# The second half's channels in a folded order, with `w1` copied once into that order in DRAM

## The chip, the cores and the metric

The kernel runs on one core of one Trainium2 chip. The metric is the time of one execution on the device in microseconds (us), the median of several runs. An execution that the hardware profiler recorded gives the profile; it has a time of its own.

## The reference

One transformer block on x of 2048 rows and 512 channels, all in float32. A vector `c` gives six modulation vectors of 512 channels: shift, scale and gate for each of the two halves.

```python
mod = (_silu(c) @ w_mod).reshape(c.shape[0], 6, 1, -1)
sa, ca, ga, sb, cb, gb = (mod[:, 0], mod[:, 1], mod[:, 2], mod[:, 3], mod[:, 4], mod[:, 5])
h = _layernorm(x, axis=-1) * (1 + ca) + sa
x = x + ga * _A_ref(h, A_wqkv, A_wo)          # linear attention, 32 heads of 16
h = _layernorm(x, axis=-1) * (1 + cb) + sb
x = x + gb * _B_ref(h, B_w1, B_b1, B_w2)      # mish(h @ w1 + b1) @ w2
```

`w1` is 512 x 1792, `w2` 1792 x 512. The first half ends with `x1 = x + ga * attention`. The second half is a layer norm of x1, two matrix products with Mish between them, and an addition to x1.

## The kernel before

**Tiling.** Rows are cut into four blocks of 512 (`b` 0 to 3), each of four tiles of 128 rows (`t`). A tile has 128 partitions and 512 columns. Channels are cut into four chunks of 128 (`j`). Every float32 operand of a product is split into a high and a low part of reduced precision, and a product is three matmuls (high by high, high by low, low by high). Most products are Strassen-like: of a 2 x 2 partition of the operands seven products are made from sums and differences (`m1` to `m7`, or `a11 b11`, `s1 t1` and so on), so VectorE makes many sums and low parts, and ScalarE the high parts.

**Stages.** From the start to about 120 us: layer norms of the blocks of x, `k` for blocks 0 to 3 (`k_unit`), and the Gram products (`g_unit`). SyncE's queue is an in-order list of loads: those of x for blocks 2 and 3 come from `load_x` in the loop `for b in range(1, NB)`, and block 3 goes through DRAM (`xd`) and back as 32 x 32 squares (`load_squares`, `y_x`). Then `q` (`q_sevens`), during which `mod_side` loads rows of `w_mod` (L155, two loads a step) and reduces each on VectorE against the activated `c` three steps later (`mod_col`, L232): column i of `mc` is the modulation of 128 channels. Rows 8 to 15 of the 24 tiles are loaded singly, 16 to 23 in pairs in the order 20 to 23, 16 to 19. Then attention (`attend`, whose reciprocals `rden` go through DRAM), `o_unit`, and x1 is stored to DRAM as `x1d` (L920).

In these parts instructions are emitted in an order fixed by `tick`, one step of every running helper per unit of TensorE's work; each engine executes its own list in order.

**The second half**, from about 187 us on, is emitted by `drive`. It keeps a main stream (pairs of products with `w1`, Mish after them) and a fill stream (`unit`, products with `w2`). All other work is jobs with due times. `drive` models every engine's clock, picks the job that can start first, and among those the one due first; the table `T` holds lead times, due times and costs. A DMA job without a fixed queue goes to SyncE or POOL, whichever the model finds free first. The order of the instructions is thus fixed when the kernel is built, and a change of `T` changes it.

**Ways of the data in the second half.** Blocks 0 and 1 are normalized on ScalarE (`norm_first`, `norm_each`) and turned by TensorE (`transpose_f`, `tp_op`). Blocks 2 and 3 are normalized in place (`norm_job`), stored to DRAM (`to_dram`, tiles `nd`), read back as squares into `yd` (`squares_job`, L1727) and turned by VectorE, which transposes 32 x 32 blocks (`turn_job`). Here `x1d` and `nd` have the shape [4, 512, 128]: chunk by chunk, so a row of a chunk is 512 bytes, and one row of a square is a run of 32 numbers, 128 bytes:

```python
yield (y[32 * c:32 * (c + 1), :].rearrange("q (m r) -> q m r", r=32),
       bass.AP(tensor=d.tensor, offset=d.offset + 512 * P * j0 + 32 * c, ap=[[P, 32], [32 * P, n], [1, 32]]))
```

The results have channels on partitions. They go three ways. For blocks 0, 1 and the first column of the second pair (block L = 2) `result_job` gates them (L1618), transposes them on VectorE into `turned` (L1629), and POOL adds them into `x1d` by four accumulating DMAs a job (L1635). `copy_out` (L1695) then copies a finished block from `x1d` to `out`. For block 3 `load_r` reads squares of x1 into `rq` (L1594), VectorE adds the transposed result (`rows_half`, L1660), and squares go straight to `out` (L1664). The last product, `m3` of block 2, is made in row order: VectorE multiplies it by the gate and adds it to `rows01`, rows of `x1d` loaded at L1892, and POOL stores them (L1928). Each engine's list is in order, so an instruction that waits for a DMA holds up what stands behind it, for example the low parts at L1270.

`w1` is loaded in `rows` (L797, the first two groups) and `rows_job` (L1288), `w2` in `w2_blocks`, `blocks_job` and `sums_job`; splits and differences of `w2` are stored to DRAM (`w2d`, `w2t`) and read again in `right_job` (L1446). Tiles named `wt_m` are these.

Of the kernel before, what the change touches and what calls it, by code (L numbers as in the profile page):

```python
# [8 lines left out]
F32 = mybir.dt.float32  # L9
F32R = mybir.dt.float32r  # L10
AF = mybir.ActivationFunctionType
ALU = mybir.AluOpType
# [17 lines left out]
 'urgent': 3.1,  # L30
 'store_later': 10.8,
 'row_lead': 12.6,
 'columns': 94.0,
 'column_lead': 27.7,
 'rows_early': 12.0,
 'lead_a': 4,
 'lead_l': 14,
 'lead_r': 14,
# [4 lines left out]
 'blocks_early': 13.3,  # L43
# [3 lines left out]
 'early_at': -0.3,  # L47
 'norm_due': 62.5,
# [10 lines left out]
 'left_early': 19.1,  # L59
 'right_due': 2.0,  # L60
 'right_early': 13.2,
 'sum_due': 1.0,
 'sum_early': 11.2,
 'pace_a': 5.6,
 'pace_l': 3.2,
 'pair_l': 16.4,
 'seq_0': 'ABCD.E.FG',
 'seq_l': 'AB.CD.E.F.G.',
 'copy_due': 10.0,
 'result_due': 5.0,  # L70
 'soon': 10.2,
 'r_due': 5.3,
 'out01': 54.8,
 'sum_store': 8.1,
 'half_due': 8.9}

@with_exitstack
def block_kernel(ctx: ExitStack, tc: tile.TileContext, x, wqkv, wo, w1, b1t, w2, c, wmodt, out):
# [18 lines left out]
    def f32(t):  # L97
        return t.bitcast(F32)

# [53 lines left out]
    def load_wmod(i):  # L153
        wm[i] = sb(f"wm_{i}")
        sp.dma_start(wm[i], wmodt[P * i:P * (i + 1), :])  # L155
# [138 lines left out]
    def strips(d, t):  # L294

        return d[:, P * t:P * (t + 1), :].rearrange("j p r -> p j r")
# [13 lines left out]
    def strip_squares(y, d, j0):  # L310

        n = y.shape[1] // 32
        for c in range(4):
            yield (y[32 * c:32 * (c + 1), :].rearrange("q (m r) -> q m r", r=32),
                   bass.AP(tensor=d.tensor, offset=d.offset + 512 * P * j0 + 32 * c, ap=[[P, 32], [32 * P, n], [1, 32]]))
# [363 lines left out]
    def w2_blocks(g):  # L679
# [8 lines left out]
        act.activation(first[:, 0, :], r[0][:, 0:H], AF.Copy)  # L688
        act.activation(h, r[1], AF.Copy)
        yield  # L690
        dve.tensor_tensor(first[:, 1, :], r[0][:, 0:H], f32(first[:, 0, :]), op=ALU.subtract)
        dve.tensor_tensor(l, r[1], f32(h), op=ALU.subtract)
# [98 lines left out]

    def rows(g, wait):

        r = [sb(f"w1p_{g}_{i}", F32, (P, 4, P)) for i in range(2)]
        for i in range(2):
            f = 2 * g + i
            sp.dma_start(r[i], w1[:, P * f:P * (f + 1)].rearrange("(k p) f -> p k f", p=P))  # L797
# [25 lines left out]
    op_rows, rows_d = {}, {}  # L823

    early_rows = [rows(g, 3 * g + 1) for g in range(2)]

    for b in range(1, NB):
# [89 lines left out]
    def x1_store(b, t, queue=pool):  # L917
        if b not in x1d:
            x1d[b] = drp.tile([4, 512, P], F32, name=f"x1d_{b}")
        queue.dma_start(strips(x1d[b], t), xt["r", b, t].rearrange("p (j r) -> p j r", r=P))  # L920
# [15 lines left out]
    def norm_first(t):  # L936
# [9 lines left out]
        ln_apply("n", 0, t, xt["r", 0, t], v, act)  # L946

    def norm_each(b, t):
# [15 lines left out]
        ln_apply("n", b, t, xt["r", b, t], v, act)  # L964
# [139 lines left out]
    LATE = T['late']  # L1104
    QUEUE = {SP: sp, POOL: pool, ACT: act}
# [173 lines left out]
    def rows_job(g, due, l=0):  # L1279
# [5 lines left out]
        def load(q, i):  # L1285
            r[i] = sb(f"w1p_{l}_{g}_{i}", F32, (P, 4, P))
            f = 2 * g + i
            q.dma_start(r[i], w1[:, P * f:P * (f + 1)].rearrange("(k p) f -> p k f", p=P))  # L1288
# [66 lines left out]
    def blocks_job(g):  # L1355
# [12 lines left out]
        def upper(i):  # L1368
            if i == 0:
                st[0] = sb(f"b11_{g}", F32R, (P, 2, H))  # L1370
                act.activation(st[0][:, 0, :], r[0][:, 0:H], AF.Copy)
            else:
                st[1] = sb(f"b2_{g}_0", F32R)
                act.activation(st[1], r[1], AF.Copy)

        def lower(i):
            if i == 0:
                dve.tensor_tensor(st[0][:, 1, :], r[0][:, 0:H], f32(st[0][:, 0, :]), op=ALU.subtract)
                right[0, "m1", g] = [st[0][:, k, :] for k in range(2)]
            else:  # L1380
                st[2] = sb(f"b2_{g}_1", F32R)
                dve.tensor_tensor(st[2], r[1], f32(st[1]), op=ALU.subtract)
# [15 lines left out]
    def sums_job(g):  # L1398
# [13 lines left out]
        def diff(n):  # L1412
            if n == 0:
                t[0], t[1] = [sb(f"t{m}_{g}") for m in (12, 34)]
            b11, b12, b21, b22 = [v[:, c:c + H] for v in (r[0], r[1]) for c in (0, H)]
            t1, t2, t3, t4 = t[0][:, 0:H], t[0][:, H:D], t[1][:, 0:H], t[1][:, H:D]
# [167 lines left out]
    def load_r(L, n):  # L1584
# [4 lines left out]
        for c in range(4):  # L1589
            def go(q, c=c):  # L1590
                if c == 0:
                    alloc()
                sq, rows_ = list(strip_squares(rq[L, n], x1d[L + n], 0))[c]
                q.dma_start(sq, rows_)  # L1594
            yield dma_(go, [("rq", L, n)] if c == 3 else (), size=2 * LATE)

# [15 lines left out]
    def result_job(L, place, n, c, us, needs, frees=()):  # L1612
# [13 lines left out]
        def turn_(i):  # L1626
            if turned[L, n] is None:
                turned[L, n] = big.tile([P, 4 * 512], F32, tag="Y", name=f"turned_{L}_{n}", bufs=YS)
            dve.transpose(turned[L, n][:, 1024 * c + 512 * i:1024 * c + 512 * (i + 1)], q[i])  # L1629

        for i in range(2):
            yield d_(lambda i=i: turn_(i))
        both = turned[L, n][:, 1024 * c:1024 * (c + 1)]
        for k, (sq, rows_) in enumerate(strip_squares(both, x1d[L + n], 2 * c)):
            yield dma_(lambda q, sq=sq, rows_=rows_: q.dma_start(rows_, sq, accum_op=ALU.add),  # L1635
                       [("sum", L, n, c)] if k == 3 else (), queue=POOL)


    def rows_half(L, place, c, i, us, keep):
# [15 lines left out]
        v = lambda: rq[L, 1][:, 512 * (2 * c + i):512 * (2 * c + i + 1)]  # L1655
# [4 lines left out]
        yield d_(lambda: dve.tensor_tensor(v(), v(), q[1], op=ALU.add), needs=[("rq", L, 1)])  # L1660
# [32 lines left out]
    def copy_out(q, b, c0, c1):  # L1693

        q.dma_start(out_rows(b)[:, P * c0:P * c1].rearrange("p (j r) -> p j r", r=P),  # L1695
                     x1d[b][c0:c1].rearrange("j p r -> p j r"))
# [272 lines left out]
```

## Time and profile before

| what | us |
|---|---|
| median of 3 runs | 492.26 |
| lowest and highest of them | 487.68, 492.45 |
| the profiled execution's own time | 495.81 |
| its span, first to last instruction | 494.1 |
| TensorE busy | 474.2 |
| VectorE busy | 418.3 |
| ScalarE busy | 321.1 |
| POOL busy | 177.5 |

The span is cut into 40 slices on the page, each 12.35 us. TensorE's clock was granted in full but for short stretches (mean 0.986). The DMA engines moved 97.24 MB in 115200 packets, 66641 of them under 512 bytes. PE is TensorE, PEld its weight loads, DVE VectorE, ACT ScalarE, SP SyncE; a name with a q behind it is that engine's queue of DMA issues. A line such as `PE m L128 <- DVE l_m_5l L1270: 7.9, 1, 7.9` says that TensorE's instruction of line 128 that writes `m` waited for VectorE's of line 1270 that writes `l_m_5l`: 7.9 us in total, once, the longest 7.9. In a stretch of time stand its length, then each engine's busy time in it with the number of its instructions, the granted clock, the DMA engines' busy share and the rate in GB/s; where transfers overlap on an engine the share can pass 1. A row of the DMA issues ends with the size of one and the median time from issue to landing.

### The profile page before, as it was taken

Reading aid. Unit: us, or ns where it says so; the run is one execution under the profiler, and the core shown is the slowest. Engines: PE = TensorE matmul, PEld = TensorE weight load, DVE = VectorE, ACT = ScalarE, POOL = GpSimd, SP = SyncE. Lnnn points to the kernel's source line nnn. Section 1 sums busy time; section 2 is a strip of 40 time slices with the busy share of each in tenths; the row PEclk is TensorE's granted clock in tenths of the full one; section 3 lists DMA queues with packets and bytes.
Section 4 is the critical chain, followed back from the end, with each engine's and each line's share of the span. In section 5 each row is a group of like instructions: output and inputs, shape, how many; then the busy total and the mean of one; then the engine's idle time right before and its main releaser. Section 6 shows DMA issues by size and latency. Waiting matters only on the chain.

```text
span 494.1 us, 7316 instructions
## 1 busy us (share of the span) xinstructions
PE 474.2 (96%) x2300; PEld 387.7 (78%) x2300; DVE 418.3 (85%) x818; ACT 321.1 (65%) x583; POOL 177.5 (36%) x245
## 2 busy tenths in 40 slices
PE   8999999999999999999999999989999999999936
PEld 6778887877877888888888778868888888888835
DVE  7989988999789798998888799968975689899734
ACT  6768586756445979779889696655565648443400
POOL 4583320000113431345421235522312266862722
PEclk9999999999999999999999999989999999999969
DMA  8705597145784536579989769983234399999996
GB/s 310 286 2 122 176 151 234 43 129 171 263 197 126 167 108 229 182 265 358 276 241 274 252 203 217 302 295 121 71 122 146 92 246 218 272 284 218 242 129 135
DMA packets 115200, 97.24 MB, mean 197 GB/s; under 512 B 66641, under 2 KB 89049, under 8 KB 115162
## 3 DMA queue, kind: packets, MB, share of 16 engines
q0 software_dynamic: 38672, 44.06, 39.3%
q1 hardware_dynamic: 72120, 51.93, 36.7%
q10 hardware_dynamic: 4370, 0.79, 0.9%
q8 instruction: 18, 0.29, 0.3%
q14 instruction: 20, 0.16, 0.1%
HBM read 65.81 MB, written 31.46 MB: 197 GB/s over the span
## 4 chain that ended last, share of the span: by engine, by line
PE 59%; DMA 16%; DVE 9%; issue 6%; ACT 5%; POOL 3%; SPq 2%; ACTq 0%; POOLq 0%; DVEq 0%
PE p_a L1487 15%; DMA x1d<-turned 6%; PE p_s L1487 6%; PE pa L1572 5%; PE pc L1572 3%; PE o L128 3%; PE o L126 3%; PE pq_a L464 3%; PE o L127 3%; DMA wt_m<-w2t 2%; SPq L322 2%; PE pd L1572 2%; DMA w2t<-t_5l 2%; DMA w1p<-in_w_dram 1%; PE pk L128 1%
## 5 line engine op out<-in xcount | busy, mean ns | idle before, releaser
L1446 POOL DMA_DIRECT2D wt_m<-w2t x35 | 27.6, 965 | 54.8 <-PE p_a L1487 10.6
L1511 ACT ACTIVATE u_a<-c_a,b1c 128x512 f32<-128x512 f32 x42 | 30.2, 718 | 16.3 <-DVE c_a L1508 16.3
L1635 POOL DMA_DIRECT2D x1d<-turned x24 | 34.9, 2468 | 15.7 <-DVE turned L1629 9.9
L1502 ACT ACTIVATE u<-p_a 128x512 f32<-128x512 f32 x42 | 24.9, 593 | 24.0 <-PE p_a L1487 23.7
L1508 DVE TENSOR_TENSOR c_a<-p_s,u 128x512 f32<-128x512 f32 x28 | 19.2, 685 | 11.1 <-PE p_s L1487 6.2
L1446 POOL DMA_DIRECT2D wt_m<-w2d x17 | 15.7, 1063 | 15.6 <-PE pa L1572 9.2
L920 POOL DMA_DIRECT2D x1d<-r x16 | 12.3, 769 | 24.1 <-DVE r L924 15.3
L895 POOL DMA_DIRECT2D rden_d<-rden x2 | 1.4, 714 | 48.2 <-DVE rden L893 48.2
L1461 DVE TENSOR_TENSOR u_a<-u_a,u_a 128x512 f32<-128x512 f32 x28 | 18.1, 681 | 0.0
L256 POOL TENSOR_TENSOR rs_n<-rs_n,half 128x1 f32<-128x1 f32 x16 | 9.9, 634 | 17.8 <-DVE rs_n L282 9.5
L355 ACT ACTIVATE e_k<-pk 128x512 f32<-128x512 f32 x15 | 8.9, 591 | 10.7 <-PE pk L128 10.6
L1288 POOL DMA_DIRECT2D w1p<-in_w_dram x12 | 10.4, 864 | 9.9 <-PE p_a L1487 5.9
L1607 ACT ACTIVATE U<-pa,mc 128x512 f32<-128x512 f32 x10 | 6.8, 681 | 10.9 <-PE pa L1572 10.6
L907 DVE SCALAR_TENSOR_TENSOR q<-q,rd 128x512 f32<-128x512 f32 x16 | 10.5, 684 | 3.8 <-DMA rd<-rden_d 3.8
L256 POOL TENSOR_TENSOR rs_x<-rs_x,half 128x1 f32<-128x1 f32 (+1 forms) x10 | 7.8, 783 | 15.8 <-DVE rs_x L251 14.6
L367 POOL DMA_DIRECT2D ku<-ku x8 | 7.1, 886 | 17.1 <-DVE ku L358 17.1
L358 DVE SCALAR_TENSOR_TENSOR ku<-e_k,relu_k 128x512 f32<-128x512 f32 x15 | 10.7, 712 | 3.0 <-ACT relu_k L356 2.9
L358 DVE SCALAR_TENSOR_TENSOR q<-e_q,relu_q 128x512 f32<-128x512 f32 x16 | 10.7, 685 | 2.1 <-ACT relu_q L356 2.1
L1508 DVE TENSOR_TENSOR c_a<-p_a,u 128x512 f32<-128x512 f32 x14 | 9.6, 683 | 3.2 <-PE p_a L1487 2.1
L1539 ACT ACTIVATE u_a<-p_a,b1c 128x512 f32<-128x512 f32 x14 | 9.6, 683 | 4.1 <-PE p_a L1487 3.6
L1660 DVE TENSOR_TENSOR rq<-rq,t 128x512 f32<-128x512 f32 x4 | 2.6, 675 | 9.5 <-DMA rq<-x1d 9.5
L232 DVE SCALAR_TENSOR_TENSOR wm<-wm,sc_row 128x512 f32<-128x512 f32 x16 | 10.5, 676 | 0.0
(1504 smaller groups left out, 1898.3 us busy)
## 6 DMA issues: line engine op xcount, KB each, us to landing
wt_m<-w2t POOLq DMA_DIRECT2D x35, 256.0 KB, 6.4
wm<-in_wmodt_dram SPq DMA_DIRECT2D x24, 256.0 KB, 5.1
wt_m<-w2t SPq DMA_DIRECT2D x17, 256.0 KB, 8.0
wt_m<-w2d POOLq DMA_DIRECT2D x17, 256.0 KB, 6.6
r<-in_x_dram SPq DMA_DIRECT2D x16, 256.0 KB, 3.2
x1d<-r POOLq DMA_DIRECT2D x16, 256.0 KB, 3.1
w2d<-b SPq DMA_DIRECT2D x16, 256.0 KB, 7.2
x<-in_x_dram SPq DMA_DIRECT2D x15, 256.0 KB, 4.7
```

The costliest lines, as they stand in the source:

```text
L126: pe.matmul(o, st[0], mv[0], start=start, stop=False)
L128: pe.matmul(o, st[1], mv[0], start=False, stop=stop)
L256: pool.tensor_tensor(y, y, half[:, lo:hi], op=ALU.pow)
L358: dve.scalar_tensor_tensor(dst, e, 1.0, r, op0=ALU.min, op1=ALU.add)
L1446: q.dma_start(f32(v), (w2d if src == "w2d" else w2t)[g][:, :, part, :])
L1461: dve.tensor_tensor(get(d), u, v, op=o)
L1487: pe.matmul(p, st, mv, start=onto is None and c == 0 and i == 0, stop=c == 1 and i == 2, skip_group_check=onto is not None)
L1502: act.activation(t["u", n], t["pa"], AF.Copy)
L1508: dve.tensor_tensor(t[key], t[p], t["u", n], op=ALU.add)
L1511: act.activation(u, t[key], AF.Mish, bias=b1c[:, f:f + 1])
L1572: pe.matmul(o, st[:, cs], mv, start=not onto and n == 0 and k == 0, stop=n == G - 1 and k == 2, skip_group_check=onto)
L1635: yield dma_(lambda q, sq=sq, rows_=rows_: q.dma_start(rows_, sq, accum_op=ALU.add), [("sum", L, n, c)] if k == 3 else (), queue=POOL)
```

## The change

Natural channel 128 c + 32 x + r (c and x from 0 to 3, r from 0 to 31) gets the place 128 x + 32 c + r: the folded order. Chunk x of the second half then holds, on partition 32 c + r, channel 128 c + 32 x + r.

- `x1d` and `nd` become plain [512, 512] tensors in natural order, stored in rows of 2 KB. A load of squares takes, for one c, 128 consecutive channels of each row: 512 bytes a run, 512 runs a load (2048 before), and the four chunks lie beside each other in each partition.
- Sums: for blocks 0 and 2 each `result_job` adds its two chunks, runs of 256 bytes, 512 a DMA; for block 1 the second of the two jobs adds all four chunks, runs of 512 bytes. 20 accumulating DMAs take the place of 24.
- Block 3: `rows_half` stores to `out` in four DMAs of 512-byte runs after the last of its four additions, in place of sixteen of 128-byte runs, each four after their own addition.
- The last product's rows: whole rows of `x1d` (four loads and four stores of 256 KB, with the second half of each row's columns, in folded view, added to). The rows now need both sums of block 2, and the copy of that block's first 256 columns to `out` falls away.
- `copy_out` copies 1 MB from one plain tensor to another.
- ScalarE and VectorE read and write through views that fold: the normalized blocks 0 and 1, the splits and differences of `w2`, the last rows.
- The modulation of the second half (loads `wm` 12 to 23) is read from `w_mod` in folded order, four groups of 32 rows a load.
- `w1` is copied in DRAM into `w1d` with its rows folded: four copies on SyncE's queue, one in each step of the loop's first turn (b = 1), right behind the load of a tile of x of block 3; `rows` and `rows_job` load from `w1d`.
- `T` has new values (one, `add`, is new: the modelled cost of a sum).

```diff
+    def nat(t, h=None):
+        v = t.rearrange("p (c x r) -> p x c r", c=4, r=32)
+        return v if h is None else v[:, 2 * h:2 * h + 2]
+    def lin(t):
+        return t.rearrange("p (x c r) -> p x c r", c=4, r=32)
+    def chunk(y, x):
+        return y.rearrange("q (m s) -> q m s", s=P)[:, :, 32 * x:32 * (x + 1)]
...
     def load_wmod(i):
         wm[i] = sb(f"wm_{i}")
-        sp.dma_start(wm[i], wmodt[P * i:P * (i + 1), :])
+        if i < 12:
+            sp.dma_start(wm[i], wmodt[P * i:P * (i + 1), :])
+        else:
+            r0 = 512 * (i // 4) + 32 * (i % 4)
+            sp.dma_start(wm[i], bass.AP(tensor=wmodt.tensor, offset=wmodt.offset + 512 * r0,
+                                        ap=[[512 * P, 4], [512, 32], [1, 512]]))
...
-            nd[key, b] = drp.tile([4, 512, P], F32, name=f"{key}d_{b}")
-        queue.dma_start(strips(nd[key, b], t), v.rearrange("p (j r) -> p j r", r=P))
+            nd[key, b] = drp.tile([512, D], F32, name=f"{key}d_{b}")
+        queue.dma_start(nd[key, b][P * t:P * (t + 1), :], v)
...
+    def strip_squares(y, d, c, lo=0, hi=P):
+        return (y[32 * c:32 * (c + 1), :].rearrange("q (m s) -> q m s", s=P)[:, :, lo:hi],
+                d[:, P * c + lo:P * c + hi].rearrange("(m q) s -> q m s", q=32))
...
+    w1d = drp.tile([D, F], F32, name="w1d")
+    def fold_rows(c, queue):
+        queue.dma_start(w1d.rearrange("(k c r) f -> c k r f", c=4, r=32)[c],
+                        w1.rearrange("(c k r) f -> c k r f", c=4, r=32)[c])
...
             if b + 2 < NB:
                 load_x(b + 2, t)
...
+            if b == 1:
+                fold_rows(t, sp)
...
-        ln_apply("n", b, t, xt["r", b, t], v, act)
+        ln_apply("n", b, t, nat(xt["r", b, t]), lin(v), act)
...
-            dve.transpose(turned[L, n][:, 1024 * c + 512 * i:1024 * c + 512 * (i + 1)], q[i])
+            dve.transpose(chunk(turned[L, n], 2 * c + i), q[i])
...
-        for k, (sq, rows_) in enumerate(strip_squares(both, x1d[L + n], 2 * c)):
-            yield dma_(lambda q, sq=sq, rows_=rows_: q.dma_start(rows_, sq, accum_op=ALU.add),
-                       [("sum", L, n, c)] if k == 3 else (), queue=POOL)
+        if n and c:
+            return
+        lo, hi = (0, P) if n else (64 * c, 64 * (c + 1))
+        for k in range(4):
+            def put(q, k=k):
+                sq, rows_ = strip_squares(turned[L, n], x1d[L + n], k, lo, hi)
+                q.dma_start(rows_, sq, accum_op=ALU.add)
+            yield dma_(put, [("sum", L, n, c)] if k == 3 else (), [("t", L, n, 1)] if n else (), queue=POOL, size=ADD)
...
-        for n in range(4):
+        for n in range(4) if c == 0 and i else ():
             def put(queue, n=n):
-                sq, rows_ = list(squares(v(), out_rows(L + 1), H * c + P * i))[n]
+                sq, rows_ = strip_squares(rq[L, 1], out_rows(L + 1), n)
                 queue.dma_start(rows_, sq)
-            yield dma_(put, queue=(SP, ACT)[c])
+            yield dma_(put, (), [("v", 0, 0), ("v", 1, 0), ("v", 1, 1)], queue=(SP, ACT)[n % 2])
...
-                    for t in range(2):
-                        r0 = P * (2 * i + t)
-                        q.dma_start(rows01[i][:, t, :].rearrange("p (j r) -> p j r", r=P),
-                                     x1d[L][2:4, r0:r0 + P, :].rearrange("j p r -> p j r"))
-                add_job(iter([dma_(lambda q: copy_out(q, L, 0, 2), (), [("sum", L, 0, 0)])]), now[0] + 20)
+                    q.dma_start(rows01[i], x1d[L][P * i:P * (i + 1), :])
...
-                            q.dma_start(out[512 * L + P * t:512 * L + P * (t + 1), H:D], rows01[t // 2][:, t % 2, :])
+                            q.dma_start(out[512 * L + P * t:512 * L + P * (t + 1), :], rows01[t])
```

Of `T`, among others: `blocks_early` 13.3 to 19.3, `row_lead` 12.6 to 15.5, `lead_l` 14 to 16, `lead_r` 14 to 13, `left_early` 19.1 to 16.4, `sum_early` 11.2 to 14.0, `norm_due` 62.5 to 60.3, `pair_l` 16.4 to 15.1, `half_due` 8.9 to 7.8, `r_due` 5.3 to 5.5, and `seq_l`, the order of products and fills in the last seven pairs, from `AB.CD.E.F.G.` to `AB.CD.E.FG..`.

More of the change, by code (lines that the diff above doesn't have):

```diff
@@ L46 @@
  'early_due': 96.7,
- 'early_at': -0.3,
- 'norm_due': 62.5,
+ 'early_at': -1.0,
+ 'norm_due': 60.3,
  'norm_at': 18.7,
@@ L918, in x1_store @@
         if b not in x1d:
-            x1d[b] = drp.tile([4, 512, P], F32, name=f"x1d_{b}")
-        queue.dma_start(strips(x1d[b], t), xt["r", b, t].rearrange("p (j r) -> p j r", r=P))
+            x1d[b] = drp.tile([512, D], F32, name=f"x1d_{b}")
+        queue.dma_start(x1d[b][P * t:P * (t + 1), :], xt["r", b, t])
     def o_post(p, b, t):
@@ L1592, in go @@
                     alloc()
-                sq, rows_ = list(strip_squares(rq[L, n], x1d[L + n], 0))[c]
-                q.dma_start(sq, rows_)
-            yield dma_(go, [("rq", L, n)] if c == 3 else (), size=2 * LATE)
+                q.dma_start(*strip_squares(rq[L, n], x1d[L + n], c))
+            yield dma_(go, [("rq", L, n)] if c == 3 else (), size=LATE)
     def out_rows(b):
@@ L1882, in fill_stream @@
                 for b in range(2):
-                    add_job(iter([dma_(lambda q, b=b: copy_out(q, b, 0, 4),
-                                       (), [("sum", 0, b, c) for c in range(2)])]), now[0] + T['out01'])
+                    add_job(iter([dma_(lambda q, b=b: copy_out(q, b),
+                                       (), [("sum", 0, 0, 0), ("sum", 0, 0, 1)] if b == 0 else [("sum", 0, 1, 0)],
+                                       size=8 * LATE)]), now[0] + T['out01'])
             if l == L and (name, g) == ("m6", ORDER[L][0]):
```

103 lines of the change are left out of this document (48 added, 55 removed).

## The prediction

> **What bounds the kernel now.** I read the head of the page, then the waits of TensorE, then stretches of time around each wait, then each engine's own order at those places.
>
> ```profile
> span 494.1 us, 7316 instructions
> PE 474.2 (96%) x2300; PEld 387.7 (78%) x2300; DVE 418.3 (85%) x818; ACT 321.1 (65%) x583; POOL 177.5 (36%) x245
> PE m L128 <- DVE l_m_5l L1270: 7.9, 1, 7.9
> PE pc L1572 <- DVE l_m_0l L1270: 2.1, 1, 2.1
> PE o L128 <- DVE qs_2l L140: 1.0, 1, 1.0
> ```
>
> TensorE is busy for 96%. All that can be won without taking matmuls away is its 494.1 - 474.2 = 19.9 us of idle time, and what the clock loses after it. One wait is 7.9 us, one 2.1, one 1.0. The stretches (columns: length, busy time of PE, PEld, DVE, ACT, POOL with counts, granted clock, DMA share, GB/s):
>
> ```profile
> 326.50:329.40 2.90, 0.78 (x5) 0.32 (x3) 0.69 (x1) 2.76 (x5) 0.72 (x1) 1.00 1.04 373
> 329.40:333.44 4.04, 4.04 (x10) 2.85 (x11) 2.61 (x5) 0.63 (x1) 1.14 (x2) 0.58 0.53 170
> 360.00:380.00 20.00, 20.00 (x90) 16.55 (x89) 12.59 (x22) 13.06 (x23) 4.74 (x7) 1.00 0.35 111
> 471.60:479.40 7.80, 0.00 (x0) 0.00 (x0) 1.92 (x4) 0.00 (x0) 0.27 (x1) 0.61 0.88 115
> 479.40:483.63 4.23, 4.21 (x19) 4.21 (x20) 4.23 (x8) 0.00 (x0) 2.63 (x4) 0.50 1.00 201
> 483.63:489.20 5.57, 5.56 (x46) 5.36 (x45) 2.41 (x7) 0.00 (x0) 1.69 (x3) 1.00 0.94 183
> 489.20:494.10 4.90, 0.00 (x0) 0.00 (x0) 0.85 (x2) 0.00 (x0) 0.54 (x1) 0.98 0.11 39
> ```
>
> After each stop the clock is granted by half for a while: 19 matmuls take 4.2 us at 0.50, where 46 like them take 5.57 at 1.00, so 19 cost 2.3; 1.9 us more are lost. Likewise 10 matmuls take 4.04 us at 333, against 90 in 20.00 us, 2.2 for ten; 1.8 lost. The last stop thus costs 7.9 + 1.9 = 9.8 us, the one at 327 2.1 + 1.8 = 3.9. Elsewhere, as from 360 to 380, TensorE has no hole. The last 4.9 us are the last tile's way out.
>
> What makes the last stop? VectorE's and SyncE's orders:
>
> ```profile
> 467.30 0.71 DVE L1649 SCALAR_TENSOR_TENSOR q<-pa,mc,T 128x512 f32<-128x512 f32 x1
> 477.48 0.69 DVE L1660 TENSOR_TENSOR rq<-rq,t 128x512 f32<-128x512 f32 x1 [9.47 <-DMA rq<-x1d]
> 478.71 0.65 DVE L1270 TENSOR_TENSOR l_m_5l<-u_a,l_m_5h 128x512 fp32r<-128x512 f32 x1
> 441.27 28.21 SPq L1594 DMA_DIRECT2D rq<-x1d  x4
> 466.70 11.88 DMA x1d<-turned
> ```
>
> TensorE wants `l_m_5l`. It needs nothing of `rq`, but stands behind L1660 on VectorE, which waits 9.47 us for `rq`. Four loads of `rq` keep SyncE's queue for 28 us: 2048 runs of 128 bytes each, while the sums `x1d<-turned`, 1024 runs each, share the DMA engines.
>
> **The change, part by part.**
>
> ```profile
> ku<-ku POOLq DMA_DIRECT2D x8, 256.0 KB, 4.6
> w1p<-in_w_dram SPq DMA_DIRECT2D x12, 256.0 KB, 5.3
> x1d<-turned POOLq DMA_DIRECT2D x24, 128.0 KB, 9.1
> x1d<-r POOLq DMA_DIRECT2D x16, 256.0 KB, 3.1
> out_dram<-rows POOLq DMA_DIRECT2D x4, 128.0 KB, 2.8
> rows<-x1d POOLq DMA_DIRECT2D x4, 128.0 KB, 3.4
> 464.28 5.48 POOL L1635 DMA_DIRECT2D x1d<-turned  x4 [1.30 <-DVE turned L1629]
> 479.13 2.90 POOL L1892 DMA_DIRECT2D rows<-x1d  x4 [9.36 <-DMA x1d<-turned]
> 490.41 0.54 POOL L1928 DMA_DIRECT2D out_dram<-rows  x1 [1.98 <-DVE rows L1925]
> ```
>
> Loads of `rq`: 512 runs of 512 bytes. By run count the 28.2 us of issue become 7.1 and the last lands about 441.3 + 7.1 + 5.3 (the `w1p` row, 512-byte runs) = 454; with no gain from longer runs it stays at 477. VectorE comes to L1660 at 468.0, so the stop goes if more than 9.5 of the 28.2 us go: a third saved, 9.4, all but does it. Taken: gone, -9.8.
>
> Sums: 24 issues of 1024 runs become 20 of 512 (16 of 256 bytes, 4 of 512). The nearest rows are the 128-byte sums (9.1 us for 128 KB) and the accumulation `ku` in 2 KB runs (4.6 for 256 KB, 2.3 for 128); 256 bytes lie nearer the first row. I take 5 to 6. Some run ahead of the stop at 327, which comes through a buffer that a store still holds. Bounds: 0 to -3.9; taken half, -2.0.
>
> Squares of `n` (L1727), stores of `n` and `x1` and copies to `out` keep their place and get fewer runs; TensorE waits for none of them: 0. Folded views on ScalarE and VectorE move as many elements; no row shows such a view, but the stage from 190 on is TensorE's (the 360 row: VectorE 12.6 of 20), so a tenth more on each would stay covered: 0.
>
> The tail: the four last stores carry 256 KB where 128 were. By the two rows (3.1 against 2.8) +0.3. Their rows now also wait for both halves of the sums; the last sums are issued from 464.3 and land at 478.6 (466.70 + 11.88). At half that flight they land near 473; four `rows` loads, 2.9 us of issue and 3.4 of flight, are there by 480, about when TensorE would end (489.2 - 9.8 = 479.4): 0. The four additions into `rq` now leave in four stores of 256 KB (sixteen of 64 before), none before the last addition is done; what queues behind that on SyncE and ScalarE is nothing else, and with VectorE free from 468 on it is over before TensorE's end: 0. The 512 KB copy of the third block's first half to `out` falls away, off every path: 0.
>
> `w1d` and `wm`: four copies (0.92 MB each, with x(3,1) to x(3,3) between them on SyncE's queue), and loads `wm` 12 to 23, whose DRAM side now has an outermost dimension of 4. What that costs is seen at `rden_d`, the one DMA here with 4 outermost, which runs alone from 180.6 to 181.8; beside it `wm` loads as they are now:
>
> ```profile
> 121.00:122.00 1.00, 1.00 (x7) 0.81 (x6) 0.98 (x2) 0.97 (x2) 0.00 (x0) 1.00 1.06 408
> 180.60:181.80 1.20, 1.20 (x8) 1.03 (x7) 1.20 (x4) 0.00 (x0) 0.93 (x1) 1.00 0.23 53
> 179.02 0.57 SPq L895 DMA_DIRECT2D rden_d<-rden  x1
> 119.00 0.80 SPq L155 DMA_DIRECT2D wm<-in_wmodt_dram  x2
> 121.40 0.80 SPq L155 DMA_DIRECT2D wm<-in_wmodt_dram  x2
> 122.77 0.86 SPq L155 DMA_DIRECT2D wm<-in_wmodt_dram  x2
> 124.99 0.88 SPq L155 DMA_DIRECT2D wm<-in_wmodt_dram  x2
> 137.15 0.69 DVE L232 SCALAR_TENSOR_TENSOR wm<-wm,sc_row 128x512 f32<-128x512 f32 x1
> 138.98 0.69 DVE L232 SCALAR_TENSOR_TENSOR wm<-wm,sc_row 128x512 f32<-128x512 f32 x1
> 141.13 0.69 DVE L907 SCALAR_TENSOR_TENSOR q<-q,rd 128x512 f32<-128x512 f32 x1 [1.25 <-DMA rd<-rden_d]
> 142.69 0.69 DVE L907 SCALAR_TENSOR_TENSOR q<-q,rd 128x512 f32<-128x512 f32 x1 [0.87 <-DMA rd<-rden_d]
> ```
>
> A share of 0.23 is 4 engines of 16. So a folded `wm` load gets a quarter of 408 GB/s, 102, and 256 KB take 2.6 us instead of 0.64, one after another on the same four. From 120.6 (issue at 119.0, and 1.6 from issue to first byte as at `rden_d`, 179.0 to 180.6), eight `wm` loads and the four `r` loads between them need 8 x 2.6 + 4 x 0.64 = 23.4 us: the last lands at 144.0, and VectorE wants it at 139.0, 5.0 us earlier. `rd` loads of POOL use the same engines at 135 to 143: 4 x 256 KB on eight engines (8 outermost, so by the same step half of 408 GB/s) are up to 5 us; half, 2.6. So 7.6 late, of which 1.25 + 0.87 replace waits for `rd`: 5.5 reach `qs_2l`, on which TensorE already waits 1.0, and the half clock adds 1.9: +7.4. Bounds: 2.9 (no `rd`, no half clock) to 9.8 (all of `rd`).
>
> The Trainium skill ("DMA: Bandwidth & Descriptors", section "Why a DMA increments its semaphore by 16 and not by 1") has the rule: a DMA uses the largest number of engines up to 16 that divides the slowest dimension of both its patterns. By that rule it is 4 here too, and the row agrees; without it, at 16 engines, the +7.4 would be 0.
>
> The copies of `w1`, early:
>
> ```profile
> 20.00:40.00 20.00, 19.78 (x95) 16.08 (x94) 17.30 (x36) 14.35 (x28) 12.68 (x22) 1.00 0.09 31
> 51.74 0.69 DVE L247 BATCH_NORM_STATS2 st_x<-x 128x6 f32<-128x512 f32 x1
> ```
>
> DMA is all but idle from 20 on. On four engines one copy is 0.92 MB / 102 GB/s = 9.0 us. x(3,3) stands behind three: 20 + 27 + 3 x 0.64 = 49, wanted by VectorE at 51.7. It fits by 2.7 us; two accumulations `ku` (4.6 each) on the same engines meanwhile could make it 6.5 late. Bounds 0 to 8.4 with the half clock; taken +1.0, nearer the fit.
>
> New plan times move the order from 187 on. With TensorE full there they can win little more than the 3.9; ±2 in the range.
>
> Sum on the profiled execution's 495.8 us: -9.8 - 2.0 + 0.3 + 7.4 + 1.0 = -3.1, 492.7. The median of the runs is 492.26, 0.9928 of the profiled time; by that factor: **489.2**.
>
> **The rivals.** A measurement here tells about 1% from no change.
>
> *The columns hide.* If `wm` lands in time (the four engines free of `rd`, or VectorE behind anyway), 7.4 and 1.0 fall away and 327 goes whole: -9.8 - 3.9 + 0.3 = -13.4, by the same factor **479**. For it: VectorE idles 2 us at 141; against: the row with 0.23.
>
> *The folded copies hold up the start.* x(3,3) late by 6.5 us holds VectorE in order at 51.7, with the splits that TensorE needs behind it; with the half clock 8.4 instead of 1.0: +4.3 in all, 500.1, by the factor **496.5**, over the 492.26 of before; with the upper bound at `wm` too, 498.9. It decides when three copies need more than 30 us on their engines. For it: 49 against 51.7; against: TensorE had no wait there, and the DMA idles.
>
> *The sums do not get shorter.* If a run's price follows its bytes, 2048 runs of 256 bytes last as long as 4096 of 128. The sums land at 478.6 again, the last `rows` load at 479.1 + 2.9 + 3.4 = 485.4, and with two additions behind it the last store leaves at some 486.4, 4 us before its 490.4 instead of 9.8: -4 + 0.3 + 7.4 + 1.0 = +4.7, by the factor **496.9**. The change then doesn't do what it says for the sums. For it: 256 is nearest to 128; against: `ku` at 2.3.
> The Trainium skill's same page (section "Specifications") puts the full rate at 512 bytes and more, with read-modify-write below; by that the 256-byte sums would stay slow, and no run here has shown it yet.
>
> **How the numbers follow.** Forecast 0.42, columns hide 0.30, copies 0.18, sums 0.10. The forecast's own range, 483 to 494 by the bounds of `wm` and the 2 us of plan, is faster by over 1% (under 487.3) in a quarter, 0.11, slower in 0.03, and within 1% in the rest, 0.28. Columns hide: faster, 0.29, or within, 0.01. Copies and sums: they stand at the edge of 1% (497.2): slower in 0.16, with the bounds of `wm` above them, within in 0.12. Faster 0.40, within 0.41, slower 0.19. For 8 in 10 the range takes in most of the second and third case: 478.5 to 498.
>
> **What would show it.** Right: L1660 without a wait and no stop after 471; `rq` issued in 7 to 12 us; `x1d<-turned` under 6 us to landing; VectorE standing at L232 between 137 and 147 for `wm`, and TensorE before `o` near 150. Wrong: no wait at L232 (479), a wait at L247 before 52 (496.5), or `rows` waiting for `x1d<-turned` beyond 480.

## The result, and the profile after

The changed kernel takes **503.76 us** (median of four runs, 503.02 to 506.18), the kernel before beside it 491.73 (487.68 to 492.45). The ratio is 1.027, with a 95% interval of 1.0204 to 1.0337: slower, and beyond the predicted range, which ended at 498. The profiled execution took 503.02 us with a span of 501.3 (495.81 and 494.1 before). The head of its page, and TensorE's waits:

```profile
span 501.3 us, 7291 instructions
PE 473.3 (94%) x2300; PEld 387.2 (77%) x2300; DVE 418.6 (84%) x818; ACT 322.1 (64%) x583; POOL 160.0 (32%) x240
DMA packets 74000, 101.43 MB, mean 202 GB/s; under 512 B 23233, under 2 KB 46921, under 8 KB 73866
```
```profile
PE gb_ps L529 <- DVE rden L910: 10.1, 1, 10.1
PE gacc L139 <- DVE pk_2l L154: 4.6, 1, 4.6
...
PE pd L1591 <- DVE t_4l L1289: 0.9, 1, 0.9
```

TensorE works as long as before (473.3 against 474.2), so the whole loss is idle time. The stop of 7.9 us at the end is gone, and so is the one of 2.1 before `pc` (the 0.9 before `pd` is another product). But two new ones stand earlier: 4.6 us before `gacc` and 10.1 before `gb_ps`. Stretches of the changed kernel (columns as before: length, busy time and count of PE, PEld, DVE, ACT, POOL, granted clock, DMA share, GB/s):

```profile
40.00:60.00 20.00, 20.00 (x98) 16.73 (x97) 18.22 (x36) 15.54 (x26) 8.27 (x10) 1.00 0.71 212
75.12:80.15 5.03, 0.40 (x3) 0.00 (x1) 1.96 (x5) 0.00 (x0) 0.00 (x0) 1.00 0.74 118
151.65:162.16 10.51, 0.39 (x3) 0.01 (x2) 3.65 (x10) 1.49 (x3) 0.00 (x0) 0.68 0.41 131
162.16:165.60 3.44, 3.44 (x9) 2.76 (x10) 3.44 (x6) 0.71 (x2) 0.69 (x1) 0.50 0.54 172
478.00:486.00 8.00, 8.00 (x49) 7.10 (x48) 8.00 (x14) 1.90 (x3) 4.39 (x4) 1.00 0.92 74
488.27:496.40 8.13, 5.07 (x43) 4.86 (x41) 3.20 (x8) 0.00 (x0) 2.27 (x5) 1.00 1.00 292
```

Both kernels run 2300 matmuls. The start of the k-th in the trace of after less the start of the k-th in that of before says how far behind the changed kernel is at that place (the plan swaps a few neighbours after 187 us, which moves single values, not these). The difference between two places is what lies between them:

| up to (time in the kernel before) | behind by, us | added there | the prediction's term |
|---|---|---|---|
| 65.7, all before the first stop | -0.1 | | |
| 126.6, behind the stop at `gacc` | +5.3 | +5.4 | copies of `w1`, +1.0 |
| 198.0, behind the stop at `gb_ps` | +19.1 | +13.8 | folded `wm` loads, +7.4 |
| 324.6 | +18.4 | -0.7 | plan, within 2 |
| 340.1, behind the old stop at 327 | +14.2 | -4.2 | -2.0 |
| 482.6, behind the old last stop | +4.6 | -9.6 | -9.8 |
| 488.9, the last matmul | +4.1 | -0.5 | |
| end of the span | +7.2 | +3.1 | tail, +0.3 |

**The first stop.** VectorE, SyncE and TensorE of the changed kernel:

```profile
78.19 0.71 DVE L338 STREAM_TRANSPOSE hf_x<-y_x 128x512 f32<-128x512 f32 x1 [4.70 <-DMA y_x<-xd]
...
79.41 0.69 DVE L154 SCALAR_TENSOR_TENSOR pk_2l<-ku,pk_2h 128x512 fp32r<-128x512 f32 x1
```
```profile
67.52 8.76 SPq L333 DMA_DIRECT2D y_x<-xd  x12
```
```profile
80.15 0.67 PE L139 MATMUL gacc<-pk_2l,xn_2h 128*128 128x512 f32 x1 [4.63 <-DVE pk_2l L154]
```

TensorE wants `pk_2l`, which stands on VectorE behind the turning of x's squares (`hf_x`). The squares were asked for at 67.52; before, at 62.07:

```profile
62.07 8.64 SPq L322 DMA_DIRECT2D y_x<-xd  x14
```

They need the rows of x's last block in DRAM, four stores of POOL. The DMA issues of the changed kernel between 40 and 60 us, and then those of the kernel before (last number: median us to landing):

```profile
ku<-ku POOLq DMA_DIRECT2D x4, 256.0 KB, 12.0
xd<-x POOLq DMA_DIRECT2D x4, 256.0 KB, 7.8
```
```profile
ku<-ku POOLq DMA_DIRECT2D x4, 256.0 KB, 4.0
xd<-x POOLq DMA_DIRECT2D x4, 256.0 KB, 2.5
```

POOL issues the `xd` stores at the same time in both (from 56.9 and 57.0). What is new are the copies of `w1`. Their packets are under way from 19.3 to 58.4 us, and hardly ever more than four of them at once. In a stretch that they have nearly to themselves, the DMA share (next to last) is 0.24, four engines of sixteen:

```profile
26.00:38.00 12.00, 11.80 (x61) 9.56 (x60) 10.23 (x19) 6.71 (x12) 9.16 (x17) 1.00 0.24 100
```

**The second stop.** VectorE, then SyncE, of the changed kernel:

```profile
147.62 0.69 DVE L249 SCALAR_TENSOR_TENSOR wm<-wm,sc_row 128x512 f32<-128x512 f32 x1 [2.81 <-DMA wm<-in_wmodt_dram]
...
156.27 0.69 DVE L249 SCALAR_TENSOR_TENSOR wm<-wm,sc_row 128x512 f32<-128x512 f32 x1 [7.34 <-DMA wm<-in_wmodt_dram]
...
159.14 0.69 DVE L249 SCALAR_TENSOR_TENSOR wm<-wm,sc_row 128x512 f32<-128x512 f32 x1 [2.17 <-DMA wm<-in_wmodt_dram]
...
161.76 0.34 DVE L910 TENSOR_SCALAR rden<-den,tiny_den 128x128 f32<-128x128 f32 x1
```
```profile
124.28 1.25 SPq L171 DMA_DIRECT2D wm<-in_wmodt_dram  x2
...
128.52 6.06 SPq L171 DMA_DIRECT2D wm<-in_wmodt_dram  x2
...
138.37 3.57 SPq L171 DMA_DIRECT2D wm<-in_wmodt_dram  x2
...
145.09 7.75 SPq L163 DMA_DIRECT2D r<-in_x_dram  x1
```

From the issue of the first of the eight (rows 20 to 23, then 16 to 19) at 124.28 to the eighth's use at 159.14 are 34.9 us. Two issues that took 0.86 us before take 6.06 here, and one `r` load behind the eight 7.75: the queue itself is held up. Behind the waits stands `rden`, for which TensorE waits: by the code `den`, which `rden` is made from, and `gb_ps` share the one buffer `tp`.

### The profile page after: what moved, and what is told of

Its sections match the earlier page's. It is cut to its first block, busy times and chain, and to the rows that moved or that the text cites. A ratio compares the mean times of both kernels' runs of the same rounds, so it can differ in the third digit from the quotient of the medians.

```text
span 501.3 us, 7291 instructions
## 1 busy us (share of the span) xinstructions
PE 473.3 (94%) x2300; PEld 387.2 (77%) x2300; DVE 418.6 (84%) x818; ACT 322.1 (64%) x583; POOL 160.0 (32%) x240
## 4 chain that ended last, share of the span: by engine, by line
PE 71%; DMA 12%; DVE 8%; ACT 3%; issue 2%; SPq 2%; POOL 1%; ACTq 0%; POOLq 0%; DVEq 0%
PE p_a L1506 18%; PE pa L1591 8%; PE p_s L1506 7%; PE pc L1591 6%; DMA wm<-in_wmodt_dram 4%; PE pb L1591 4%; PE pd L1591 3%; PE pq_a L475 3%; PE gacc L139 2%; PE gacc L140 2%; PE gacc L138 2%; PE pk L140 2%; PE pk L138 2%; PE pk L139 2%; SPq L333 2%
## 5 line engine op out<-in xcount | busy, mean ns | idle before, releaser
L1465 POOL DMA_DIRECT2D wt_m<-w2t x30 | 24.5, 1009 | 45.9 <-PE pc L1591 11.5
L1527 DVE TENSOR_TENSOR c_a<-p_s,u 128x512 f32<-128x512 f32 x28 | 19.3, 690 | 15.7 <-PE p_s L1506 8.3
L1657 POOL DMA_DIRECT2D x1d<-turned x20 | 22.0, 1740 | 30.5 <-DVE turned L1647 23.7
L1465 POOL DMA_DIRECT2D wt_m<-w2d x16 | 12.6, 1054 | 18.6 <-PE p_a L1506 5.2
L273 POOL TENSOR_TENSOR rs_n<-rs_n,half 128x1 f32<-128x1 f32 x16 | 11.6, 726 | 15.6 <-DVE rs_n L299 8.8
L146 ACT ACTIVATE qs_0h<-q 128x512 fp32r<-128x512 f32 x4 | 2.5, 628 | 21.0 <-DVE q L925 21.0
L938 POOL DMA_DIRECT2D x1d<-r x16 | 9.0, 562 | 20.6 <-DVE r L942 14.0
L1625 ACT ACTIVATE U<-pa,mc 128x512 f32<-128x512 f32 x10 | 6.9, 688 | 11.4 <-PE pa L1591 11.2
L273 POOL TENSOR_TENSOR rs_x<-rs_x,half 128x1 f32<-128x1 f32 (+1 forms) x10 | 7.8, 780 | 15.8 <-DVE rs_x L268 14.6
L529 PE MATMUL gb_ps<-ident,mc 128*4 128x128 f32 x1 | 0.4, 372 | 10.1 <-DVE rden L910 10.1
```

The costliest lines, as they stand in the source:

```text
L273: pool.tensor_tensor(y, y, half[:, lo:hi], op=ALU.pow)
L1465: q.dma_start(f32(v), (w2d if src == "w2d" else w2t)[g][:, :, part, :])
L1527: dve.tensor_tensor(t[key], t[p], t["u", n], op=ALU.add)
```

## The experiments

Each run stands beside the kernel before, and ratios are to that. Only intervals apart are called a difference.

| run | us | ratio, 95% |
|---|---|---|
| before + folded `wm` loads | 505.89 | 1.0257 (1.0203 to 1.0310) |
| before + copies of `w1` | 495.74 | 1.0056 (1.0024 to 1.0088) |
| after, shorter packets | 504.23 | 1.0210 (1.0161 to 1.0258) |
| after, copies on 16 engines | 498.22 | 1.0101 (1.0055 to 1.0147) |
| after, `wm` on 16 engines | 494.69 | 1.0072 (1.0032 to 1.0112) |
| after, both on 16 engines | 487.20 | 0.9878 (0.9833 to 0.9923) |
| that, times of the plan before | 488.67 | 0.9923 (0.9890 to 0.9957) |
| that, stores by quarters | 488.49 | 0.9889 (0.9841 to 0.9937) |
| that, last rows by halves | 486.40 | 0.9853 (0.9813 to 0.9893) |
| that, both tails | 484.71 | 0.9863 (0.9793 to 0.9932) |
| the last, `wm` from two queues | 486.49 | 0.9891 (0.9856 to 0.9925) |

**Copies on sixteen engines.** The same copies with 32 rows outermost in place of the index k of 4:

```diff
-        queue.dma_start(w1d.rearrange("(k c r) f -> c k r f", c=4, r=32)[c],
-                        w1.rearrange("(c k r) f -> c k r f", c=4, r=32)[c])
+        queue.dma_start(w1d.rearrange("(k c r) f -> c r k f", c=4, r=32)[c],
+                        w1.rearrange("(c k r) f -> c r k f", c=4, r=32)[c])
```

> The changed kernel with one edit: each copy of w1 walks its 128 rows with the 32 rows of a group outermost and the four groups inside, so that its slowest dimension is 32 in place of 4; the same bytes go to the same places. Theory (DMAs with 4 outermost use 4 engines and hold up what stands behind them): the stop of TensorE before 80 us (4.6 us, and half clock after it; 5.4 us by the shift of its matmuls) goes, about 498 us. Rival (the 7.3 MB that the copies read and write cost the time, however they are spread): no change, 503 to 504. Rival (the loss lies in the second half, in the folded views and the new plan times): no change either.

Measured 498.22. The stop at `gacc` is gone, and the stores land as fast as in the kernel before:

```profile
ku<-ku POOLq DMA_DIRECT2D x4, 256.0 KB, 3.3
xd<-x POOLq DMA_DIRECT2D x4, 256.0 KB, 2.5
```

The stop at `gb_ps` stays (11.1 us). The copies' packets are over at 32.1 us in place of 58.4. So the way the copies run made the first stop.

**Shorter packets, still four engines.** The packet records of the changed kernel hold 64 packets of 57,344 bytes, 2.1 us each: 32 neighbouring rows lie together on both sides and move eight to a packet. On sixteen engines the copies have no such packets either, so that run changed two things. Here the rows of `w1d` are made longer, so that rows don't merge:

```diff
-    w1d = drp.tile([D, F], F32, name="w1d")
+    w1d = drp.tile([D, F + P], F32, name="w1d")
...
-        queue.dma_start(w1d.rearrange("(k c r) f -> c k r f", c=4, r=32)[c],
+        queue.dma_start(w1d[:, 0:F].rearrange("(k c r) f -> c k r f", c=4, r=32)[c],
```

> The changed kernel with the rows of the folded copy of w1 128 numbers longer in DRAM, so that the copies cannot be merged into runs longer than a row: still four engines, packets of at most 7,168 bytes. If the length of the packet is what holds the other queues up (each of their packets waits for one of 2.1 us): the early stop shrinks from 4.6 us to under 1.5 and the time is 498 to 499.5, as with the copies on sixteen engines (498.2). If it is the occupation of four engines over 40 us: the stop stays and the time is 503 to 504.

Measured 504.23: no better. The packets of the copies are now of 7,168 bytes, as with sixteen engines; the counts on the pages of these two runs (padded first) tell it, 70 packets of 8 KB and more in each against 134 in the changed kernel:

```profile
DMA packets 74449, 101.43 MB, mean 202 GB/s; under 512 B 23234, under 2 KB 46922, under 8 KB 74379
```
```profile
DMA packets 74496, 101.43 MB, mean 204 GB/s; under 512 B 23281, under 2 KB 46969, under 8 KB 74426
```

The stores in the padded run, and its stop:

```profile
ku<-ku POOLq DMA_DIRECT2D x4, 256.0 KB, 8.3
xd<-x POOLq DMA_DIRECT2D x4, 256.0 KB, 6.7
```
```profile
PE gacc L139 <- DVE pk_2l L154: 4.0, 1, 4.0
```

My theory of the long packet falls. Short ones let `ku` through sooner (8.3 against 12.0), but the four engines still have 3.7 MB to move and are occupied until some 62 us, beyond the `xd` stores. That each of these stores has a share on the four is argued, not shown: the traces don't tell the engines apart. The Trainium skill ("DMA: Bandwidth & Descriptors", section "Queues, rings and completion order") says that an engine takes turns between queues packet by packet. The `ku` rows agree in direction; for `xd` the shorter packet was worth 1.1 us of the 5.3.

**The copies alone**, in the kernel before, with no reader.

> The kernel before with the four copies of w1 into the folded order added and nothing that reads them, so only the copies' own cost is seen. Theory (the copies' packets of 57,344 bytes hold up GpSimd's queue on four of the sixteen engines, so x3's rows reach DRAM late, and TensorE stops near 75 us): 5 to 6 us over the kernel before, with a stop of TensorE of 4 to 5 us between 70 and 85 us and a wait of VectorE at hf_x of 4 to 5 us. Rival (the early stop came from the new plan times or the new stores and only showed up beside the copies): within 1.5 us of the kernel before, no such stop.

Measured 495.74, ratio 1.0056: some 3 us over the kernel before, where 5 to 6 were expected. The stop itself came as expected, in the waits of that run:

```profile
PE m L128 <- DVE l_m_5l L1278: 7.6, 1, 7.6
PE gacc L127 <- DVE pk_2l L142: 4.4, 1, 4.4
...
PE pc L1580 <- DVE l_m_0l L1278: 0.8, 1, 0.8
```

But of the 5.2 us that it was behind at 89 us, 3.9 were left at 198, 0.7 at 340 and 0.04 at the last matmul of the profiled execution. Later stops that end with a transfer took it back: the one at 327 fell from 2.1 us to 0.8, and the half clock behind it went. In the changed kernel these stops are gone, so nothing takes it back: it and the run with the copies on sixteen engines, 5.8 us apart at 126.6, are still 4.9 apart at the last matmul. A stop's price depends on what waits later.

**`wm` on sixteen engines**: four loads of 32 partitions in place of one with the group of rows outermost.

```diff
-            sp.dma_start(wm[i], bass.AP(tensor=wmodt.tensor, offset=wmodt.offset + 512 * r0,
-                                        ap=[[512 * P, 4], [512, 32], [1, 512]]))
+            for c in range(4):
+                sp.dma_start(wm[i][32 * c:32 * (c + 1), :], wmodt[r0 + P * c:r0 + P * c + 32, :])
```

> The changed kernel with one edit: each folded load of a modulation tile (12 to 23) is four loads of 32 partitions, each with 32 outermost, in place of one with 4 outermost. SyncE issues 36 DMAs more, some 0.4 us each. Theory: VectorE's waits for these loads (14.4 us) go, TensorE's stop at 152 us (10.1, and half clock) with them; by the shift of the matmuls 12 us, so about 491 to 492 us. Rival (the loads come late because SyncE's queue is full, or because POOL's loads compete): the waits stay in part, 498 or more; more issues make it worse.

Measured 494.69, some 3 us above the expectation. The stop at `gb_ps` fell from 10.1 to 3.6 us, not to nothing: VectorE still waits 5.9 us for one of these loads. Between 126.6 and 198 the matmuls lose 5.5 us in place of 13.8. In the profiled executions of the versions below, with the same loads, it is 2.7 to 5.5, and the stop 0.8 to 3.6, so this rest differs from run to run.

**The folded `wm` loads alone**, in the kernel before. The modulation of the second half is then applied to the wrong channels; the work is the same.

> The kernel before with one edit: modulation tiles 12 to 23 are loaded in folded order, with 4 outermost, as in the changed kernel; nothing else is folded, so the second half's modulation is applied to the wrong channels, and the work is the same. Theory: VectorE waits for the loads and TensorE stops near 150 us; some 10 us slower than before, 500 to 503 us, since without the copies the loads start 5 us earlier. Rival (the loads cost only behind the copies, or not at all): 491 to 493.

Measured 505.89, more than expected. Nothing else was changed, and the stop at `gb_ps` is the same 10.1 us:

```profile
PE gb_ps L523 <- DVE rden L897: 10.1, 1, 10.1
PE m L128 <- DVE l_m_5l L1275: 7.1, 1, 7.1
```

Its matmuls are 0.75 us ahead at 126.6 and 14.6 behind at 198.

**Both on sixteen engines.**

> Both edits together: copies of w1 and modulation loads over 16 engines. Theory: both stops go and the gain at the last stage stays (the stop of 7.9 us before the last product and its half clock were gone in the changed kernel): 503.8 - 5.4 - 12 = 486 us, 1% under the kernel before. Rival (something else in the second half costs what was lost): not under 492.

Measured 487.20, ratio 0.9878: faster than the kernel before by 1.2%. No wait of TensorE is above 1.1 us, and its last matmul starts 13.2 us earlier than before. So the idea of the change pays; two access patterns made it lose. The two repairs together are worth 0.039 of the ratio (1.027 to 0.9878).

**The plan before**: the same kernel with the old table `T` (`add` kept).

> The version with both folded loads on sixteen engines, with the plan times of the kernel before. Theory (the stop in the last stage went because the sums move fewer packets, not because of where the plan puts them): no stop of TensorE over 2 us after 460, and 486 to 489.5. Rival (the new plan times carry it): a stop of 3 to 8 us at the last stage or at 327 comes back, and 490 to 495.

Measured 488.67. No stop over 2 us comes back after 198; at the old last stop 9.5 us are won as with the new table, and at 327 4.2. It is not the plan times, then, but the new layout; how much of it is the sums and how much the loads of `rq` wasn't separated. With the old table SyncE issues all four loads of `rq` in 8.3 us, where the kernel before took 28.2. The interval overlaps that of the new table, so what the new times are worth isn't told.

**The tail.** In the version with both repairs 9.3 us pass from the start of the last matmul to the end of the span (5.2 before). Two ways of handing bytes over earlier, each as the kernel before has it. First, block 3 stored by quarters of the channels, each after its own addition, in runs of 128 bytes:

```diff
-        for n in range(4) if c == 0 and i else ():
+        for n in range(4):
             def put(queue, n=n):
-                sq, rows_ = strip_squares(rq[L, 1], out_rows(L + 1), n)
+                sq, rows_ = strip_squares(rq[L, 1], out_rows(L + 1), n, 32 * x, 32 * (x + 1))
```

> The version with both folded loads on sixteen engines, and with the last block's stores as the kernel before has them: each quarter of the channels is stored right after its own addition, in runs of 128 bytes, in place of four stores of 512-byte runs after the last addition. Theory (two megabytes of stores bunch after the last additions, and the end waits for their bytes; TensorE's end to the end of the span is 9.3 us, 5.2 before): 484 to 485.5, with 6 to 7 us from TensorE's end to the end of the span. Rival (the bunch is set by the rows' stores alone, or 128-byte packets cost what the earlier start saves): 486.5 to 488.

Second, the last rows' loads and stores cut to the second half of the channels, the first half copied to the output as soon as it is summed:

```diff
-                    q.dma_start(rows01[i], x1d[L][P * i:P * (i + 1), :])
+                    q.dma_start(rows01[i], x1d[L][P * i:P * (i + 1), :].rearrange("p (c s) -> p c s", s=P)[:, :, 64:])
```

> The version with both folded loads on sixteen engines, and with the last rows' first half of the channels copied to the output from DRAM as soon as it is summed, as the kernel before has it, so that the loads and stores of the last rows move 0.5 MB each instead of 1 MB. Theory (the end waits for the bytes of the bunched stores): 484.5 to 486. Rival (packets of 256 bytes cost more than half of those of 2 KB, so that fewer bytes take as long): 487 to 488.5.

And both:

> The version with both folded loads on sixteen engines, with both changes to the tail together: the last block stored in quarters right after each addition in runs of 128 bytes, and the last rows' first half of the channels copied early. If the end waits for bytes that are handed over late (each change alone took 1 to 2 us off the 9.3 us from TensorE's end to the end of the span): 6 to 7 us there, and 484.5 to 486. If the small packets of the one take back what the other saves: 7 to 8.5 us there, and 486 to 488.

From the last matmul to the end they take 8.4, 7.4 and 6.7 us. By the medians that is 488.49, 486.40 and 484.71, with intervals that overlap each other and that of the version without them (487.20): the tail got shorter in the profiled executions, and the total isn't told apart. The first missed its expectation (484 to 485.5), the second lies between its two (484.5 to 486, and 487 to 488.5), the third met it. The profiled execution with quarters had lost 2.8 us more by 198, ahead of its edit, with a stop of 3.6 us at `gb_ps` against 0.8. And the loads of the last rows, which the quarters should have helped, are waited for longer there, as the waits of VectorE show (first without, then with quarters):

```profile
DVE rows L1942 <- DMA rows<-x1d: 2.3, 2, 1.5
```
```profile
DVE rows L1943 <- DMA rows<-x1d: 4.0, 2, 3.6
```

**What is left at `wm`.** In all these versions VectorE still waits 4.6 to 5.9 us for one of the folded loads. Half of them on GpSimd's queue:

```diff
-                sp.dma_start(wm[i][32 * c:32 * (c + 1), :], wmodt[r0 + P * c:r0 + P * c + 32, :])
+                (sp if c < 2 else pool).dma_start(wm[i][32 * c:32 * (c + 1), :], wmodt[r0 + P * c:r0 + P * c + 32, :])
```

> The version with both changes to the tail, with half of the 48 loads of the folded modulation rows issued on GpSimd's queue in place of SyncE's. What is left of the price in the modulation stage there is 2.7 to 5.5 us (the shift of the matmuls between 127 and 198 us of the kernel before, over the versions with the loads on sixteen engines), beside a wait of VectorE of 4.6 to 5.9 us for the last of these loads. If SyncE's issues (48 at some 0.46 us, 22 us in one row, with the loads of x between them) set when the last one lands: the wait goes under 2 us and the time is 481 to 483.5. If the bytes on the engines set it, or GpSimd's reciprocals then wait behind its new issues: 484 to 487.

Measured 486.49, with a wait of 6.2 us: taking half of the issues from SyncE did not shorten it. What sets it stays open.

## Why the prediction was wrong, step by step

**Right.** The last stop: -9.8 predicted, -9.6 measured, with no wait at the addition (L1683) for `rq`. Part of the way there was another: the plan gave three of the four loads of `rq` to POOL, which issued them from 454.7 to 461.3, and they took 15.2 to 17.4 us to land where 5.3 were taken. Those three were there by 478.7 at the latest (460.67 + 0.65 + 17.4), and VectorE came to the addition at 482.1: the gain had as little as 3 us to spare, where the prediction had 14 (454 against 468.0). The sums: 5 to 6 us were taken for 128 KB. By the DMA issues sixteen of them land at a median of 6.9 us, more than taken, but less than the 9.1 of before; below that row the last ones, from the chain of waits:

```profile
x1d<-turned POOLq DMA_DIRECT2D x16, 128.0 KB, 6.9
```

```profile
478.52 2.02 POOL x1d L1657 x2
480.55 4.92 DMA x1d<-turned
```

The last flight took 11.88 us before. Landing times also depend on what else moves (2.5 and 7.8 us for the `xd` stores), packet times less. A packet of a sum took 36 ns at 128 bytes, 46 at 256 and 65 at 512 (medians), so a byte costs a third less at 256 than at 128. So the rival "the sums do not get shorter" is out. The prediction drew from the Trainium skill ("DMA: Bandwidth & Descriptors", section "Specifications") that the 256-byte sums would stay slow: they are still slower by the byte than at 512, but quicker than at 128. The stop at 327 was taken at half its bound (-2.0), and all of it went (-4.2 against the bound -3.9).

**Wrong: the folded `wm` loads**, +7.4 in place of +13.8, by far the largest miss. The mechanism was right (four engines; a quarter of the rate; VectorE in order behind). The step that failed is "eight `wm` loads and the four `r` loads between them need 8 x 2.6 + 4 x 0.64 = 23.4 us", with half of `rd` added. With 1.6 us to the first byte that is 25.0 us from the first issue to the eighth's landing, and 27.6 with `rd`; measured are 34.9 to its use. VectorE was to get the eighth 7.6 us late and got it 14.8 late (159.14 against 139.0 and the 5.3 of the first stop). A load by itself cost what was taken: 128 packets of 84 ns, four at a time, are 2.7 us, and from 131 to 137 some four are under way at a time. The sum let the queue issue freely and the packets run without a gap. In the trace pairs of issues take 6.06 and 3.57 us, and from 149 to 153, while POOL's `rd` loads land, only 1.9 packets of SyncE's queue are under way on average. That `rd` takes these engines from `wm`, as the prediction had it, would fit, but no trace tells the engines apart: the share of each cause stays open. The bound above, 9.8, came from the same sum and was no bound.

The waiting instruction was another, too. The prediction let 5.5 us reach `qs_2l` and TensorE at `o`; that wait is 1.0 as before. TensorE stood earlier in its order, at `gb_ps`, since `rden` too stands behind the last of these loads: it was idle for 10.1 us, and the half clock behind it took 3.44 us for 9 matmuls. The run with these loads alone gives +15.4 from 126.6 to 198, so the term stands by itself.

The Trainium skill's rule for the number of engines (same page, section "Why a DMA increments its semaphore by 16 and not by 1") agrees with these runs: the copies and the loads with 4 outermost ran four packets at a time, and with 32 outermost the stop of 4.6 us went and the one of 10.1 fell to 3.6.

The same section says that on the queues of SyncE and ScalarE it is always the lowest-numbered engines. The traces here can't tell.

**Wrong: the copies of `w1`**, +1.0 in place of +5.4; inside the bounds (0 to 8.4), but by another road. The step was "x(3,3) stands behind three ... It fits by 2.7 us". It did fit: VectorE's statistics of it run at 51.7 in both. What the step left out is the fourth copy, until some 58 us, and POOL's stores of `xd` at 57 to 59, whose way over DRAM ends at VectorE's turning of the squares. The rival "the folded copies hold up the start" had the right sign and a price of 8.4 us for it, with the wrong waiting instruction; its 496.5 is still 7 us short, by the `wm` loads. The time of one copy, 9.0 us, was about right (four rounds of packets of 2.1 us). The share of 0.71 between 40 and 60 (0.64 in the kernel before) hides it: an average over sixteen engines doesn't show that four of them have a queue.

**Wrong: the tail**, +0.3 in place of +3.1. Two steps failed. One is "By the two rows (3.1 against 2.8) +0.3": the four last stores took 6.9 us to land (median).

```profile
out_dram<-rows POOLq DMA_DIRECT2D x4, 256.0 KB, 6.9
```

The other is "with VectorE free from 468 on it is over before TensorE's end: 0". VectorE is not free: it works through the whole stretch from 478 to 486. Its last two additions need a product that TensorE ends at 483.3, and end at 488.3, 4.8 us before the last matmul; then 1 MB of `rq` leaves at once, beside 1 MB of rows loaded and 1 MB stored. The step looked at what queues behind these stores and not at what moves beside them. The stretch from 488.27 to 496.40 has a DMA share of 1.00. That the stores hold each other up there is read from it; the runs on the tail shortened it but did not settle the total.

Together: +5.4 + 13.8 - 0.7 - 4.2 - 9.6 - 0.5 + 3.1 = +7.3, against 7.2 measured on the spans.

## What to carry to other kernels

Look at the outermost dimension of both sides of every DMA that a new layout makes, before its bytes: an index of 4 there made 256 KB and 0.9 MB transfers run four packets at a time and cost 3.9% here, where 32 rows outermost move the same bytes and the change wins. Don't price such a transfer by bytes over rate alone: eight loads took 34.9 us here where that sum gave 25.0. Then list every other transfer that will use those engines meanwhile, whatever queue issues it, and follow each to the instruction that stands in order behind it. And when a stop is removed, the earlier losses that it took back come into the total.

## What the runs showed of the hardware that was not expected

- Copies that ran four packets at a time (DMA share 0.24) made another queue's transfers late: 256 KB stores of POOL landed after 7.8 us in place of 2.5, although TensorE, VectorE and POOL ran as before until then. With the copies on sixteen engines it was 2.5 again.
- Packets of 7,168 bytes in place of 57,344, still four at a time, changed little (6.7 us).
- A loss of 5.2 us early in the kernel before was all but gone at its last matmul (0.04 us in the profiled execution; over all runs the ratio was 1.0056).
- Moving half of 48 loads of 64 KB from SyncE's queue to POOL's won nothing that could be seen (486.49 and 484.71, intervals overlapping).
- An accumulating DMA's packets took 36 ns at 128 bytes, 46 at 256 and 65 at 512: twice the bytes cost 1.3 to 1.4 times the time.
